# Stage one of the first two batches as plain products over 94 input rows, in place of folded rows of 120

## The chip, the cores and the metric

One core of one Trainium2 chip. The metric is the device time of one execution in microseconds; the kernel before took 2572.51 us, the median of three runs (2570.09 to 2573.17). Less is better.

## The reference

An input x of 8 batches x 3008 positions x 256 channels, float32, goes through a frequency-domain layer and then through a two-matrix feed-forward layer:

```python
X = np.fft.rfft(x, axis=1)
Yr = Xr @ w_r - Xi @ w_i + b_r
Yi = Xr @ w_i + Xi @ w_r + b_i
Yr = np.sign(Yr) * np.maximum(np.abs(Yr) - 0.01, 0.0)     # Yi likewise
y = np.fft.irfft(Yr + 1j * Yi, n=3008, axis=1)
h = y.reshape(24064, 256) @ w_in
out = (np.maximum(h, 0.0) ** 2) @ w_out
```

`w_r` and `w_i` are 256 x 256, `w_in` is 256 x 2048, `w_out` 2048 x 256; the last two are given in double precision and used as sums of two reduced-precision parts.

## The kernel before

**The transform.** 3008 is 64 x 47 (N1 x N2). Stage one is a transform of length 47 over n2 for each of the 64 values of n1; of the 47 outputs 24 groups g are kept, since the others mirror them. Stage two is, for each group, a product with a 128 x 128 matrix (`bm`) over n1 and the two parts (t: cosine and sine sums). Mixing with `w_r` and `w_i`, the bias, the threshold and the way back follow, group by group. Between the stages the data go through DRAM: `s1` holds the result of stage one, `s3` that of the first half of the way back.

**Folding.** In stage one x(n2) and x(47 - n2) share a cosine and differ in the sign of the sine. So the host lays 24 pairs out side by side, and a tile has 120 rows (24 pairs x 5 values of n1, M1) and 13 tiles (J) per batch. `Fwd32` (L429, batch 0) loads two tiles together, adds and subtracts the pair on DVE and POOL (`fold`, L276), multiplies the sum and the difference by the cosine and sine halves of `am32` (L444, products of 512 columns over both tiles), copies to `xe` with ACT and DVE and stores to `s1` (`store`, L282) on SP's queue. `Fwd2` (L406, batch 1) does not fold: it multiplies both members of the pair and adds in PSUM, by `am32` or by its negative `nam`, four products of 256 columns per tile, and copies with ACT over the tile that it read. `Fwd` (batches 2 to 7) folds on POOL and multiplies in split precision.

**The order of the work.**
- *Front* (L784 to L800). SP loads `am32` and the tiles of batch 0, four at first, each further one when a buffer (`big`) comes free. `awake` (L126) gives TensorE products on zeros: 6 at the start, 16 behind the last product of stage one. Behind the last store `load_mix_weights` (L134) loads the mixing weights and the first `kbb` on SP's queue, and splits the weights with ACT and DVE.
- *Units* (L819 to L839). `Unit32` is one group of batch 0: `load` reads `ka` from `s1`, `fwd` (L477) is stage two, `mix` (L491), `shrink` (threshold, `kv`), `back` (L503), `store`; the calls are staggered over five rounds. Beside them DVE and ACT convert the feed-forward weights: 16 parts of 512 KB (`Double`), of which `paced` takes parts 0 to 8 at a rate of one per 2.5 units, with `win_sums` after parts 1, 5, 9 and 13. Parts 9, 10, 12 and 13 (`BEHIND`) are loaded in the last units and converted behind them; 11, 14 and 15 (`LATE`) are converted within the first seven steps (`turns`). In rounds 12 to 18 `load_early` fetches seven tiles of batch 1 (`PRE`), whose stage one runs directly behind the units (L840), with stores on POOL's queue.
- *Main part.* A new pool `main` takes the memory of the closed ones. The first token tile's way back (`Back.mm`, banks `psfa` and `psfb`), its split into `yt`, and two more tiles of batch 1 come first. Then 384 steps follow (48 token tiles x 8), each 21 products `psh` of the first matrix and 12 products `pso` of the second. DVE combines `psh` (`mp`, `mu`, `mv`, `mc`), ACT squares and rounds, DVE or POOL takes the rest (`mg`). A planner (`Plan`, L689) places everything else of the transform into the slots between, two PSUM banks wide: the last four tiles of batch 1 (L920), the groups of batch 1 (`Pair`, from slot 14.8 on), stage one of batch 2 and on.

`then` (L574) chains the instructions of one engine in program order, `load_next` (L116) those of a DMA queue; `issue_after` puts an instruction behind another one on the same engine. Otherwise the order on an engine is set when the program is built.

## Time and profile before

| what | value |
|---|---|
| median of three runs | 2572.51 us |
| the profiled execution's own time | 2569.69 us |
| its span (first to last instruction) | 2567.9 us |
| TensorE (PE) busy | 2554.5 us, 99% |
| VectorE (DVE) busy | 1809.3 us, 70% |
| ScalarE (ACT) busy | 1369.7 us, 53% |
| GpSimd (POOL) busy | 1616.9 us, 63% |
| DMA | 244.47 MB, mean 95 GB/s |

Busy times are of the span. Products are pipelined and their ends are modelled, so a busy TensorE is not one at its peak, and a float32 product stands as two records. PEld is the weight load, SPq the queue of DMA issues that SP runs, POOLq that of POOL. A line of the order of time gives start, duration, engine, line, operation, output<-input, shape, count, and in brackets the idle time ahead of it with what ended it. "KB" of a transfer is 1024 bytes; GB/s are 10^9 bytes.

### The profile page before, as it was taken

Reading aid. Unit: us, or ns where it says so; the run is one execution under the profiler, and the core shown is the slowest. Engines: PE = TensorE matmul, PEld = TensorE weight load, DVE = VectorE, ACT = ScalarE, POOL = GpSimd, SP = SyncE. Lnnn points to the kernel's source line nnn. Section 1 sums busy time; section 2 is a strip of 40 time slices with the busy share of each in tenths; the row PEclk is TensorE's granted clock in tenths of the full one; section 3 lists DMA queues with packets and bytes.
Section 4 is the critical chain, followed back from the end, with each engine's and each line's share of the span. In section 5 each row is a group of like instructions: output and inputs, shape, how many; then the busy total and the mean of one; then the engine's idle time right before and its main releaser. Section 6 shows DMA issues by size and latency. Waiting matters only on the chain.

```text
span 2567.9 us, 47397 instructions
## 1 busy us (share of the span) xinstructions
PE 2554.5 (99%) x17140; PEld 2347.1 (91%) x17140; DVE 1809.3 (70%) x3808; ACT 1369.7 (53%) x2178; POOL 1616.9 (63%) x1604
## 2 busy tenths in 40 slices
PE   9999999999999999999999999999999999999999
PEld 6899999999999999999999999999999999999998
DVE  6887776777757876678766787667776667756554
ACT  5755555555555555555555555555555555545453
POOL 1056666676666766676666766666666666756564
PEclk9999999999999999999999999999999999999999
DMA  9633333333323332233322333223332232211010
GB/s 278 223 89 108 104 91 89 115 99 102 95 77 98 102 114 85 82 105 117 103 79 77 112 106 103 80 79 111 105 114 84 66 94 83 65 45 54 22 35 17
DMA packets 184715, 244.47 MB, mean 95 GB/s; under 512 B 20934, under 2 KB 130102, under 8 KB 184482
## 3 DMA queue, kind: packets, MB, share of 16 engines
q1 hardware_dynamic: 171442, 217.10, 27.5%
q0 software_dynamic: 13040, 24.34, 3.8%
q8 instruction: 137, 2.24, 0.4%
q14 instruction: 96, 0.79, 0.1%
HBM read 143.97 MB, written 97.39 MB: 94 GB/s over the span
## 4 chain that ended last, share of the span: by engine, by line
PE 96%; DVE 1%; POOL 1%; DMA 1%; issue 1%; ACT 0%; SPq 0%; POOLq 0%; ACTq 0%; DVEq 0%
PE pso L576 40%; PE psh L576 36%; PE psfa L576 9%; PE psfb L576 9%; PE psf L491 2%; PE psf L576 0%; PE psf L477 0%; PE psf L503 0%; DMA x<-x_in 0%; DMA xt<-x_in 0%; DVE mc L108 0%; POOL mg L111 0%; DMA w<-w_r_in 0%; PE psf L444 0%; DVE mv L576 0%
## 5 line engine op out<-in xcount | busy, mean ns | idle before, releaser
L111 POOL TENSOR_TENSOR mg<-mc,mg 128x500 fp32r<-128x500 f32 (+1 forms) x756 | 955.2, 1285 | 597.3 <-ACT mg L104 502.4
L576 PE MATMUL pso<-mg,wout 128*128 128x500 f32 (+1 forms) x4608 | 1153.6, 391 | 0.4 <-ACT mg L104 0.2
L576 PE MATMUL psh<-yt,win 128*128 128x250 f32 (+1 forms) x8064 | 1040.8, 280 | 1.0 <-DVE mc L108 0.9
L576 PEld LDWEIGHTS psh<-yt,win 128*128 128x128 f32 x8064 | 989.5, 189 | 13.2 <-PE psh L576 0.8
L576 PEld LDWEIGHTS pso<-mg,wout 128*128 128x128 f32 x4608 | 821.3, 188 | 132.5 <-POOL mg L111 1.3
L576 ACT ACTIVATE mc<-mc 128x1000 f32<-128x1000 f32 (+1 forms) x384 | 400.9, 1044 | 490.5 <-DVE mc L108 488.6
L108 DVE CUSTOM_DVE_ANT_0 mc<-psh,mv 128x500 f32<-128x500 f32 (+3 forms) x768 | 419.1, 548 | 345.0 <-PE psh L576 303.2
L104 ACT CAST mg<-mc 128x1000 fp32r<-128x1000 f32 (+1 forms) x384 | 396.5, 1032 | 20.3 <-ACT mc L576 0.4
L576 DVE TENSOR_TENSOR mv<-psh,mu 128x500 f32<-128x500 f32 (+1 forms) x384 | 260.8, 679 | 34.6 <-PE psfb L576 0.5
L105 DVE COPY mp<-psh 128x250 f32<-128x250 f32 (+1 forms) x376 | 157.0, 418 | 57.9 <-PE psh L576 37.2
L278 POOL TENSOR_TENSOR xs<-xt 120x256 f32<-120x256 f32 x156 | 112.5, 742 | 103.5 <-DMA xt<-x_in 89.2
L576 DVE TENSOR_TENSOR mu<-psh,mp 128x250 f32<-128x250 f32 (+1 forms) x384 | 160.4, 418 | 15.1 <-ACT mp L104 4.7
L108 DVE CUSTOM_DVE_ANT_0 mc<-psh,mp 128x250 f32<-128x250 f32 (+1 forms) x384 | 156.9, 408 | 0.0
L111 POOL TENSOR_TENSOR ksl<-kv,ksh 128x512 fp32r<-128x512 f32 x84 | 109.1, 1299 | 27.3 <-ACT ksh L104 20.7
L111 DVE TENSOR_TENSOR ul<-xs,uh 120x512 fp32r<-120x512 f32 x78 | 91.7, 1175 | 32.6 <-ACT uh L104 31.5
L111 POOL TENSOR_TENSOR yt<-ms,yt 128x500 fp32r<-128x500 f32 (+1 forms) x94 | 107.4, 1143 | 1.3 <-ACT yt L104 1.3
L111 POOL TENSOR_TENSOR yt<-yr,yt 128x500 fp32r<-128x500 f32 (+1 forms) x95 | 89.5, 942 | 21.3 <-ACT yt L104 17.7
L111 POOL TENSOR_TENSOR ms<-yr 128x250 f32<-128x250 f32 (+1 forms) x94 | 65.4, 703 | 52.3 <-DVE yr L563 37.0
L104 ACT CAST ksh<-kv 128x512 fp32r<-128x512 f32 x84 | 52.2, 621 | 76.1 <-DVE kv L111 76.1
L389 DVE TENSOR_TENSOR kv<-psfb,ke 64x256 f32<-64x256 f32 x184 | 77.5, 421 | 14.1 <-PE psfb L576 11.0
L111 POOL TENSOR_TENSOR kyl<-kp,kyh 128x256 fp32r<-128x256 f32 x84 | 62.4, 743 | 35.8 <-ACT kyh L104 35.6
L104 ACT CAST uh<-xs 120x512 fp32r<-120x512 f32 x78 | 48.3, 619 | 57.6 <-DMA s<-xe 40.8
(167 smaller groups left out, 2960.8 us busy)
## 6 DMA issues: line engine op xcount, KB each, us to landing
du<-s SPq DMA_DIRECT2D x112, 256.0 KB, 3.1
ka<-s SPq DMA_DIRECT2D x84, 256.0 KB, 3.5
kcm<-cm_in POOLq DMA_DIRECT2D x84, 256.0 KB, 3.1
s<-kuh SPq DMA_DIRECT2D x168, 128.0 KB, 1.7
s<-kul SPq DMA_DIRECT2D x168, 128.0 KB, 2.0
xt<-x_in SPq DMA_DIRECT2D x84, 240.0 KB, 3.5
s<-xe SPq DMA_DIRECT2D x79, 240.0 KB, 2.4
out<-mo SPq DMA_DIRECT2D x64, 250.0 KB, 3.1
```

The lines of the kernel that those rows point to most:

```text
L104: return act.copy(out=out, in_=in_)
L105: return eng.tensor_copy(out=out, in_=in_)
L108: return dve._custom_dve(TENSOR_ADD_SAT, out=out, in0=in0, in1=in1, s0=_float(0x7F7FFFFF), s1=0.0)
L111: return eng.tensor_tensor(out=out, in0=a, in1=b, op=ALU.subtract)
L278: return eng.tensor_tensor(out=out[:, :n], in0=self.xt[:, :n, 0], in1=self.xt[:, :n, 1], op=(ALU.add, ALU.subtract)[t])
L389: dve.tensor_add(out=v[64 * r:64 * r + 64, g], in0=ps[gs], in1=self.e[gs, r])
L491: nc.tensor.matmul(ps[:, :D], self.x[:, c, js], w32[j][:, c], start=n == 0, stop=n == 3)
L576: last_of[eng] = op(*args, **kwargs)
```

## The change

- Batches 0 and 1 get a stage one without pairs. The host lays x out as 96 rows (K1): two halves of n1 (32 values each) by 47 values of n2, and two rows of zeros. One 96 x 96 matrix `am` gives all 24 groups, both parts and both halves in one product. A `Block` is four n1 (JB): 96 x 1024, 384 KB, two products of 512 columns, two copies back into the tile that was read, one store. Eight blocks (NB) make a batch. `s1` of these batches has 128 rows per group in the order of part and n1, and stage two uses `bt`, the matrix `bm` with its rows in that order.
- Batch 0: all eight loads are issued at once (eight buffers `x4`, the first block in two loads); the mixing weights' loads stand behind blocks 3 and 4. ACT copies the first bank and DVE the second. Behind the store of block 1 SP loads `kbb`, behind that of block 3 part 0 of the feed-forward weights; the biases `b32` go on POOL's queue. `awake` behind the last product has 8 products in place of 16.
- Part 0 is converted ahead of the units, parts 1 to 8 one round earlier than before, and part 9 within the units (round 21); `BEHIND` is 10, 12, 13.
- Batch 1: six blocks are loaded in rounds 10 to 20 into `x4`, multiplied behind the units, copied by ACT and stored on POOL's queue; the pool `early` that holds them is closed after them. The remaining two blocks are four `Half`s of 96 x 512 behind the first way back. The planner gets no tile of batch 1, and `nam` goes.

The diff, cut to its core:

```diff
+K1, JB = 2 * N2 + 2, 4
+NB = N1 // 2 // JB
 FRONT = {
-    "a32": 1, "b32": 1, "w320": 1, "w321": 1, "big": 4, "small": 4, "ds": 1, "dw": 3, "ka": 6, "xe": 7, "x2": 4,
-    "kv": 4, "kc": 2, "kn": 2, "kx": 3, "ku": 4, "psf": 6, "x6": 7, "nam": 1, "zero": 1,
+    "b32": 1, "w320": 1, "w321": 1, "big": 4, "small": 4, "ds": 1, "dw": 3, "ka": 6, "x4": 8,
+    "kv": 4, "kc": 2, "kn": 2, "kx": 3, "ku": 4, "psf": 6, "zero": 1,
...
-    s1 = [dram.tile([G, NP1, 2, D], F32, name=f"s1_{b}") for b in range(B)]
+    s1 = [dram.tile([G, NP1, 2, D] if b > 1 else [G, 2 * N1, D], F32, name=f"s1_{b}") for b in range(B)]
...
-    am32 = const.tile([M1, 2, M1], F32, name="am32")
+    am = const.tile([K1, K1], F32, name="am")
...
-    nc.sync.dma_start(am32, a32)
+    nc.sync.dma_start(am, a96)
...
-    def load_mix_weights():
+    def load_bias():
         b32 = T("b32", [128, D], F32)
         for j, v in enumerate((b_r, b_i)):
-            with tc.issue_after(ring[5].folds[1].ins):
-                pool.dma_start(b32[64 * j:64 * j + 64, :], v.unsqueeze(0).broadcast_to([64, D]))
-        for j, w in enumerate((w_r, w_i)):
-            st = T(f"w32{j}", [128, 2, D], F32)
-            w32.append(st)
-            nc.sync.dma_start(st, w.rearrange("(c p) d -> p c d", p=128))
-        Unit32.matrix(0, "kbb", bm)
+            pool.dma_start(b32[64 * j:64 * j + 64, :], v.unsqueeze(0).broadcast_to([64, D]))
+        return b32
+
+    def load_mix(j):
+        st = T(f"w32{j}", [128, 2, D], F32)
+        nc.sync.dma_start(st, (w_r, w_i)[j].rearrange("(c p) d -> p c d", p=128))
+        return st
+
+    def split_mix():
...
             self.a = T("ka", [128, 2, D], F32)
-            load_next(self.a, s1[self.b][self.g:self.g + 2, :N1].rearrange("g n t c -> (n t) g c"))
+            src = s1[self.b][self.g:self.g + 2]
+            load_next(self.a, src[:, :N1].rearrange("g n t c -> (n t) g c") if self.b > 1 else src.rearrange("g n c -> n g c"))
             self.m = T("kb", [128, 2, 128], F32)
-            load_next(self.m, bm[:, self.g:self.g + 2])
+            load_next(self.m, (bm if self.b > 1 else bt)[:, self.g:self.g + 2])
...
-    class Fwd2(Fwd):
-        def load_early(self, after):
...
+    class Block:
+        def __init__(self, b, q):
+            self.b, self.q = b, q
+
+        def load(self, after=None):
+            self.xt = T("x4", [K1, JB, D], F32)
+            with tc.issue_after(after.ins) if after else nullcontext():
+                for j in range(0, JB, JB // 2) if not after and not self.q else (0,):
+                    js = slice(j, j + JB // 2) if not after and not self.q else slice(0, JB)
+                    self.get = nc.sync.dma_start(self.xt[:, js], x0[self.b, self.q, :, js])
+
+        def mm(self):
+            self.ps = []
+            for h in range(2):
+                ps = bank([128, 2, D])
+                self.end = nc.tensor.matmul(ps[:K1], am, self.xt[:, 2 * h:2 * h + 2], start=True, stop=True)
+                self.ps.append(ps)
+
+        def put(self, engs, queue):
+            for h, ps in enumerate(self.ps):
+                copy(engs[h], self.xt[:, 2 * h:2 * h + 2], ps[:K1])
+            rows = s1[self.b].rearrange("g (q j) c -> (g q) j c", j=N1 // 2)
+            self.last = queue.dma_start(rows[:, JB * self.q:JB * self.q + JB], self.xt)
+
+
+    class Half:
+        def __init__(self, q, h, tag):
+            self.q, self.j, self.tag = q, 2 * h, tag
+
+        def load(self):
+            self.xt = T("x2h", [K1, 2, D], F32, tag=self.tag)
+            load_next(self.xt, x0[1, self.q, :, self.j:self.j + 2])
 
         def run(self):
             ps = bank([128, 2, D])
...
-    class Fwd32(Fwd):
...
+            then(pe, pe.matmul, ps[:K1], am, self.xt, start=True, stop=True)
+            copy(act, self.xt, ps[:K1])
+            rows = s1[1].rearrange("g (q j) c -> (g q) j c", j=N1 // 2)
+            j = JB * self.q + self.j
+            nc.sync.dma_start(rows[:, j:j + 2], self.xt)
...
-            self.get = nc.sync.dma_start(self.a, s1[self.b][self.g, :N1].rearrange("n t c -> (n t) c"))
+            self.get = nc.sync.dma_start(self.a, s1[self.b][self.g])
...
-                        self.matrix(self.g + 1, "kbb", bm)
+                        self.matrix(self.g + 1, "kbb", bt)
...
-    ring = [Fwd32(0, q, 2) for q in range((J + 1) // 2)]
+    ring, second = ([Block(b, q) for q in range(NB)] for b in range(2))
...
-    pools.update(dict.fromkeys(("xe", "x2"), memory(early, "early", side="right")))
-    for f in ring[:FRONT["big"]]:
+    pools["x4"] = memory(early, "early", side="right")
+    for q, f in enumerate(ring):
+        if q in (4, 5):
+            with tc.issue_after(ring[q - 1].get.ins):
+                w32.append(load_mix(q - 4))
         f.load()
     awake(6)
+    behind = {2: lambda: Unit32.matrix(0, "kbb", bt), 4: parts[0].load}
     for r in range(len(ring) + 1):
+        at(ring, r, "mm")
         if r:
-            at(ring, r - 1 + FRONT["big"], "load")
-        at(ring, r, "mm")
-        at(ring, r - 1, "put")
-    awake(16, ring[-1].end)
-    early.close()
-    del pools["xe"], pools["x2"]
-    with tc.issue_after(ring[-1].last.ins):
-        b32 = load_mix_weights()
-    nam = T("nam", [M1, M1], F32)
-    act.mul(nam, am32[:, 1], -1.0)
+            f = ring[r - 1]
+            f.put((act, dve), nc.sync)
+            if r in behind:
+                with tc.issue_after(f.last.ins):
+                    behind[r]()
+            if r == 5:
+                with tc.issue_after(f.last.ins):
+                    b32 = load_bias()
+    awake(8, ring[-1].end)
+    split_mix()
     phase["pool"] = memory(middle, "middle", side="right")
...
-    PACED, BEHIND, LATE = 9, (9, 10, 12, 13), (11, 14, 15)
...
+    PACED, BEHIND, LATE = 10, (10, 12, 13), (11, 14, 15)
...
-    paced = [(n, (5 * n) // 2) for n in range(PACED)]
-    loads = [(max(k - 4, 3 * n - 3) if n < 2 else k - 4, parts[n]) for n, k in paced] + [(18 + j, parts[n]) for j, n in enumerate(BEHIND)]
-
-    PRE = 7
-    second = [Fwd2(1, q) for q in range(J)]
+    paced = [(0, -4)] + [(n, (5 * n) // 2 - 1) for n in range(1, PACED)]
+    loads = [(max(k - 4, -2), parts[n]) for n, k in paced[1:]] + [(18 + j, parts[n]) for j, n in enumerate(BEHIND)]
+
+    PRE = 6
+    halves2 = [Half(PRE + j // 2, j % 2, tag) for j, tag in enumerate(("xt", "xt", "xe", "mg1"))]
     for r in range(-5, len(units) + 4):
         at(units, r + 5, "load")
         at(units, r + 1, "fwd", "bins")
@@ -835,12 +838,15 @@
         for n, k in paced:
             if k == r:
                 convert(n, units[k - 4] if k > 3 else None)
...
-        if 0 <= r - 12 < PRE:
-            second[r - 12].load_early(units[min(r + 5, len(units) - 1)].get)
-    for q in range(PRE):
-        second[q].run()
+        if r >= 10 and not r % 2 and r // 2 - 5 < PRE:
+            second[r // 2 - 5].load(units[min(r + 5, len(units) - 1)].get)
+    for f in second[:PRE]:
+        f.mm()
+        f.put((act, act), pool)
     chain[nc.sync], chain[pool] = units[-1].get, last_pool
     middle.close()
+    early.close()
+    del pools["x4"]
     front.close()
...
-    nam = T("nam", [M1, M1], F32)
-    act.mul(nam, am32[:, 1], -1.0)
-    for f in second[PRE:PRE + 2]:
+    for f in halves2:
         f.load()
...
-    for c, f in enumerate(second[PRE:PRE + 2]):
-        at_bank[0] = ("psfa", "psfb")[c]
+    for c, f in enumerate(halves2):
+        at_bank[0] = ("psfa", "psfb")[c % 2]
         f.run()
...
-                old = run = None
-                for q in range(PRE + 2, J):
-                    at = 1.5 * (q - PRE - 2) + 1.0
-                    plan.job(max(at - 1.5, 0.6), second[q].load, [(old, 1)])
-                    old, run = run, plan.group(at + 1.5, second[q].run, 1, [(run, 3)])
                 plan.job(first - 0.6, pairs[1][0].load)
...
+    al = np.zeros((K1, G, 2, 2))
...
+        for r in range(2):
+            al[N2 * r:N2 * r + N2, g, 0, r], al[N2 * r:N2 * r + N2, g, 1, r] = np.cos(ang), -np.sin(ang)
...
+    xl = np.zeros((2, K1, N1 // 2, D), x.dtype)
+    xl[:, :2 * N2] = x[:2].reshape(2, N2, 2, N1 // 2, D).transpose(0, 2, 1, 3, 4).reshape(2, 2 * N2, N1 // 2, D)
...
-        "x0_in": np.concatenate([xi[0, :, :, q:q + 2].reshape(-1, 2, D) for q in range(0, J, 2)]),
-        "x_in": xi[1:].transpose(0, 3, 1, 2, 4, 5).reshape(B - 1, J, M1, 2, D),
+        "x0_in": xl.reshape(2, K1, NB, JB, D).transpose(0, 2, 1, 3, 4),
+        "x_in": xi[2:].transpose(0, 3, 1, 2, 4, 5).reshape(B - 2, J, M1, 2, D),
...
+        "bt_in": bm.reshape(G, N1, 2, 128).transpose(2, 1, 0, 3).reshape(128, G, 128).astype(np.float32),
```

## Rows read from the trace of the kernel before

**Rows 1.** The page, chain that ended last: share of the span by engine

```profile
PE 96%; DVE 1%; POOL 1%; DMA 1%; issue 1%; ACT 0%; SPq 0%; POOLq 0%; ACTq 0%; DVEq 0%
```

**Rows 2.** Windows: us, busy PE, PEld, DVE, ACT, POOL (instructions), clock, DMA share, GB/s

```profile
4.00:16.00 12.00, 11.27 (x24) 4.06 (x23) 5.64 (x9) 2.93 (x5) 5.30 (x3) 1.00 1.01 243
16.00:20.00 4.00, 3.96 (x10) 1.31 (x9) 2.00 (x5) 1.76 (x3) 3.05 (x4) 1.00 0.96 385
22.00:27.00 5.00, 5.00 (x25) 4.41 (x24) 0.00 (x0) 0.00 (x0) 0.00 (x0) 1.00 0.93 316
34.00:40.60 6.60, 6.60 (x38) 5.98 (x37) 6.34 (x16) 5.30 (x17) 0.00 (x0) 1.00 1.06 377
40.00:80.00 40.00, 40.00 (x217) 36.00 (x216) 39.09 (x91) 34.19 (x95) 0.00 (x0) 1.00 0.90 277
80.00:94.50 14.50, 13.21 (x67) 11.48 (x66) 9.12 (x22) 9.65 (x29) 0.00 (x0) 1.00 0.60 199
86.50:88.00 1.50, 1.50 (x10) 1.40 (x9) 1.03 (x3) 0.80 (x4) 0.00 (x0) 1.00 0.86 326
94.50:106.60 12.10, 12.10 (x57) 10.26 (x57) 10.97 (x25) 8.37 (x15) 3.21 (x6) 1.00 0.73 243
140.00:157.00 17.00, 16.63 (x104) 14.80 (x103) 15.50 (x25) 9.18 (x13) 6.40 (x7) 1.00 0.30 82
```

**Rows 3.** The front in order of time; last line: `ka`, issue to landing

```profile
1.11 5.43 PE L130 MATMUL psf<-zero 128*128 128x256 f32 x12 [1.11 <-POOL lam L123]
...
12.13 0.33 SPq L288 DMA_DIRECT2D s<-xe  x1
...
21.11 7.07 PE L130 MATMUL psf<-zero 128*128 128x256 f32 x32
...
26.64 1.30 SPq L467 DMA_DIRECT2D ka<-s  x3
...
30.05 1.13 PE L477 MATMUL psf<-kbb,ka 128*128 128x128 f32 x8 [1.87 <-ACT wx L104]
...
DMA to landing us min/median/max: 3.2/5.1/5.5
```

**Rows 4.** The chain in order of time: stage one of batch 1

```profile
94.71 12.10 PE psf L576 x56
```

**Rows 5.** Order of time from the last unit on

```profile
94.01 0.70 PE L503 MATMUL psf<-kv,kk 128*128 128x256 f32 x2 [1.29 <-DVE kv L111]
...
107.32 0.31 ACT L856 ACTIVATE nam<-am 120x120 f32<-120x120 f32 x1
```

**Rows 6.** DVE in order of time, two successive steps

```profile
148.29 0.42 DVE L576 TENSOR_TENSOR mu<-psh,mp 128x252 f32<-128x252 f32 x1 [0.49 <-ACT mp L104]
...
154.60 0.42 DVE L576 TENSOR_TENSOR mu<-psh,mp 128x252 f32<-128x252 f32 x1 [0.49 <-ACT mp L104]
```

**Rows 7.** One line's products in the front; groups from 94.5 to 106.8 us

```profile
L444 PE MATMUL psf<-x,am x28: 379/592/690, 6.5 to 20.9; 120*120 120x512 f32 x24, 120*120 120x256 f32 x4
...
L576 PE MATMUL psf<-x,am 120*120 120x256 f32 x42 | 10.2, 379 | 0.0
L104 ACT COPY x<-psf 120x512 f32<-120x512 f32 x6 | 3.5, 584 | 2.7 <-PE psf L576 2.7
```

**Rows 8.** DMA issues: count, KB each, median us to landing

```profile
s<-xe SPq DMA_DIRECT2D x79, 240.0 KB, 2.4
...
s<-x POOLq DMA_DIRECT2D x7, 240.0 KB, 5.8
...
du<-s SPq DMA_DIRECT2D x4, 192.0 KB, 2.7
```

**Rows 9.** Groups from 94.5 to 106.8 us: operations of the conversion

```profile
L176 DVE SCALAR_TENSOR_TENSOR df<-da,df 128x512 int32<-128x512 int32 x4 | 2.7, 686 | 0.0
L165 ACT ACTIVATE da<-dst 128x512 f32<-128x512 f32 x4 | 2.6, 678 | 0.0
...
L173 DVE TENSOR_SCALAR da<-da 128x512 f32<-128x512 f32 x4 | 1.7, 422 | 1.1 <-ACT da L165 1.1
```

More of the change, by code (lines that the diff above doesn't have):

```diff
@@ L42 @@
     "xs": 1, "xe": 1, "du": 2, "kv": 1, "kp": 1, "kq": 1, "ksh": 1, "ksl": 1, "kxl": 1, "kxh": 1, "kyh": 1, "kyl": 1, "ke": 1, "kb": 1, "yr": 1,
-    "amr": 1, "ms": 1, "mp": 1, "mu": 1, "mv": 1, "mc": 3, "nam": 1,
+    "amr": 1, "ms": 1, "mp": 1, "mu": 1, "mv": 1, "mc": 3,
 }
@@ L60, in fnet_moe @@
 @with_exitstack
-def fnet_moe(ctx: ExitStack, tc, x0, x, w_r, w_i, b_r, b_i, w_in, w_out, bm, cm, dx, a32, ar, c32, d32, out):
+def fnet_moe(ctx: ExitStack, tc, x0, x, w_r, w_i, b_r, b_i, w_in, w_out, bm, bt, cm, dx, a96, ar, c32, d32, out):
     nc = tc.nc
@@ L150, in load_mix_weights @@
             sub(dve, wx[1][:, j], w, wx[0][:, j])
-        return b32
     class Double:
@@ L273, in load @@
             self.xt = T("xt", [M1, 1, 2, D], F32)
-            load_next(self.xt[:, 0], x[self.b - 1, self.q])
+            load_next(self.xt[:, 0], x[self.b - 2, self.q])
         def fold(self, eng, out, t):
@@ L403, in back @@
             store_back(self.b, self.g + g, ps[:, :D])
-    class Fwd2(Fwd):
-        def load_early(self, after):
-            self.xt = T("x6", [M1, 1, 2, D], F32)
-            with tc.issue_after(after.ins):
-                nc.sync.dma_start(self.xt[:, 0], x[self.b - 1, self.q])
-        def add(self):
-            pass
+    class Block:
[18 more added lines that the diff above has]
+            self.last = queue.dma_start(rows[:, JB * self.q:JB * self.q + JB], self.xt)
@@ L415, in run @@
+    class Half:
[4 more added lines that the diff above has]
+            load_next(self.xt, x0[1, self.q, :, self.j:self.j + 2])
         def run(self):
             ps = bank([128, 2, D])
-            for t in range(2):
-                for i in range(2):
-                    then(
-                        pe, pe.matmul, ps[:M1, t], nam if t and i else am32[:, t], self.xt[:, 0, i],
-                        start=i == 0, stop=i == 1,
-                    )
@@ L423, in run @@
-            self.ev = self.xt
-            copy(act, self.ev[:, 0], ps[:M1])
-            self.store(nc.sync if self.q >= PRE else pool)
-    class Fwd32(Fwd):
-        alone = property(lambda self: self.q in (4, 8))
-        def load(self):
-            self.xt = T("x4", [M1, 2, 2, D], F32, tag="big")
-            src = x0[self.q * M1:(self.q + self.n) * M1].rearrange("(m n) t d -> m n t d", n=self.n)
-            self.get = nc.sync.dma_start(self.xt[:, :self.n], src)
-        def mm(self):
-            n = self.n
-            self.ps, self.folds = [], []
-            for t, eng in enumerate((dve, dve if self.alone else pool)):
-                u = T("x2", [M1, 2, D], F32)
-                self.folds.append(self.fold(eng, u, t))
-                ps = bank([128, 2, D])
-                self.end = nc.tensor.matmul(ps[:M1, :n], am32[:, t], u[:, :n], start=True, stop=True)
-                self.ps.append(ps)
-        def put(self):
-            self.ev = T("xe", [M1, 2, 2, D], F32)
-            for t, ps in enumerate(self.ps):
-                self.done = copy((act, act if self.alone else dve)[t], self.ev[:, :self.n, t], ps[:M1, :self.n])
-            self.last = self.store()
+            then(pe, pe.matmul, ps[:K1], am, self.xt, start=True, stop=True)
@@ L1003, in _consts @@
             cm[g, j, 64 + n1], cm[g, 64 + j, 64 + n1] = sg * w * s, sg * w * e * c
-    return am.reshape(M1, 2, M1), bm, cm, dm
+    return am.reshape(M1, 2, M1), al.reshape(K1, K1), bm, cm, dm
 def _r12(v):
```

4 lines of the change are left out of this document (2 added, 2 removed).

## The prediction

> **What bounds the kernel now.** I read the page first, then busy time by windows, then the order of time on each engine around the places that the diff touches. The page says that the end hangs on TensorE: 96% of the chain that ended last [rows 1]. From about 157 us on the diff touches nothing, so the question is how much earlier or later that steady part begins. Ahead of it lie four stretches with four limits.
>
> *Front, 0 to 30 us: transfers.* The DMA share is 0.93 to 1.01. Until 16 us, when almost only loads of x have moved, the rate is 243 GB/s; while the stores of stage one drain it is 385 [rows 2]. The first store is issued at 12.13 us, yet the rate rises only when the loads are through, so I take SP's queue as served in order. SP issues the first `ka` at 26.64 us, when the last store has landed, and units begin at 30.05 [rows 3].
>
> *Units, 30 to 94.7 us: TensorE,* busy 40.0 of 40 us in their middle, with DVE at 39.1 [rows 2]; one gap of 1.3 us at the end [rows 5].
>
> *Second batch's stage one, 94.7 to 106.8 us: TensorE,* 56 records in 12.10 us, 0.216 us each [rows 4]. Two more tiles run behind the first back products; then the steps start.
>
> *First steps, 113.8 to 157 us: VectorE, not TensorE.* A step's second half ends with an `mc`; then ACT can copy `mp` (one buffer), then DVE starts the next `mu`. That costs a wait of 0.49 us a step, and DVE is otherwise full: 15.5 of 17.0 us [rows 2], 6.31 us from one `mu` to the next [rows 6]. TensorE's 99% hides that here; its busy time is modelled.
>
> **The change, part by part.**
>
> *Stage one of batch 1 on TensorE.* Now 13 tiles of four products of 256 columns, two records each: 13 x 8 x 0.216 = 22.5 us. After: 16 products of 512 columns. A record of 512 columns lasts 0.592 us at the median in the front, one of 256 columns 0.379 [rows 7], of which 0.379 - 0.216 = 0.163 is the modelled tail; so 0.429 is its own, and a product 0.858 us. Where the 16 fall:
> - Six blocks in the bounding stretch: 12 x 0.858 = 10.3 against 12.1 us. **Gain 1.8 us.**
> - Four halves behind the back products: 3.43 against 2 x 1.73 = 3.46. Nothing.
> - The four tiles planned into the steps (6.9 us of TensorE) vanish where DVE is the limit. I cost this at nothing: the next `mu` waits for `mc`, not for a product. A loss is excluded, since work only goes; the most it could give is the 0.5 us of one wait.
> - `nam` is no longer built between the copies that the back products wait for: 0.31 us at 107.32 [rows 5]. **Gain 0.2 us.**
>
> The evictions of the six blocks are all ACT's, 12 x 0.58 = 7.0 us [rows 7] in 10.3. It has 8.4 us of work in that stretch now [rows 2]; six copies more add 3.5, part 9 takes away five operations of up to 0.68 [rows 9], some 2.9: 9.0, which fits, and six banks cover a late copy.
>
> *Part 9 into the units, part 0 ahead of them.* A part is on DVE three operations of 0.42 us and three of 0.69 [rows 9], 3.3 us; part 9 has four sums (0.42) and four differences (one of 0.42, three of 0.69) besides, 4.2. DVE has 5.4 us free from 80 to 94.5 us [rows 2], and part 0 leaves 3.3 us earlier in the units: 7.5 fits into 8.7, tightly. If the last units' `kv` operations queue behind it, they lose at most two of 0.69 us. The 7.5 us that DVE saves after the units bound nothing, since the six blocks use no DVE. Zero, at worst -1.4.
>
> *SP and POOL queues.* The units carry six loads of 384 KB for seven of 240 KB, and one part of 512 KB less: +0.1 MB on a stretch at 277 GB/s that reaches 377 [rows 2], wanted only at its end; zero. POOL issues six stores instead of seven. `du` still stands ahead of the halves' loads.
>
> *The front.* The folds go, but they only stood between landing and product. TensorE: the six opening products hold it until 6.5 us [rows 3]; 16 x 0.858 = 13.7 more, so its last product ends at 20.2 at the earliest, the last copy at 20.9, the last store is issued at 21.2. With the 2.4 us in which a 240 KB store lands in the main part [rows 8] that is 23.6: the floor. Over it stands what the queue must move by then: loads 3.15 (x) + 0.52 (mixing weights) + 0.04 + 0.23 (POOL's two constants) + 0.13 (biases) = 4.07 MB; then stores 3.15, `kbb` 0.26, part 0 0.52 = 3.93 MB. Stores go at 385 GB/s: 10.2 us. Loads of 96 partitions have no row; the ends are 243 (loads of x) and 377 GB/s (34 to 40.6 us, when no store is out). The nearest in row length, with no x beside it, is the lone part at 86.5 to 88 us, 4 KB rows at 326 [rows 2]; I take that. Loads from 2.0 us then end at 14.5, and the last store lands at 14.5 + 10.2 + 0.3 = 25.0; `ka` is issued 0.3 later. It lands in 3.2 us at best now [rows 3], with weights still in the queue; 192 KB on a quieter queue take 2.7 [rows 8], which I take. Units begin at 28.0. **Gain 2.0 us** (ends: 377 gives the floor, 23.6 + 3.0 = 26.6, +3.4; 243 gives 32.2, -2.2). Splitting the mixing weights hides in this wait.
>
> *TensorE's clock.* [...] The longest idle time ahead of the units is 1.9 us now, at a granted clock of 1.00. After, eight products fill 20.2 to 23.7 us and the engine idles to 28.0: 4.3 us, which no row shows. The price is between 0 and 5.43 - 12 x 0.22 = 2.8 us; units fill slowly at first, so I take 0.3.
> [...]
>
> *Sum.* 1.8 + 0.2 + 2.0 - 0.3 = 3.7 us. The profiled execution took 2569.69 us (span 2567.9 and 1.8 around it) and would take 2566.0; it lies 2.8 below the median of the runs, 2572.51, against which I predict: **2568.8 us**, 0.14% less. About 0.2%, 5.1 us, is what a measurement of this kernel can tell from no change: below 2567.4 or above 2577.7.
>
> **The rivals.**
>
> *Loads at full rate (0.36).* If x comes in at 377, TensorE is the front's limit, units start at 26.6 (+3.4), the engine idles only 2.9 us and keeps its clock. With 2.0 from batch 1: 5.4 us, 2567.1; the gap of 1.3 us at the units' end may be filled too, since the new products are in no chain: 2565.8. For it: the rate at 34 to 40.6 us. Against it: 12 us of x at 243.
>
> *96 partitions move slower (0.14).* Loads at 243 and the rest at the 316 GB/s of 22 to 27 us [rows 2]: 2.0 + 16.7 + 12.4 + 0.3 + 0.3 + 2.7 = 34.4, units 4.4 us late; 2.0 gained and up to 2.8 lost by the clock: 2574.9 to 2577.7. For it: x never came faster. Against it: stores of the same tiles did 385.
> [...]
>
> *Buffers freed late (0.11), slower.* The `early` pool, which holds x4, is now closed only after the six blocks, and tiles of the main part take its memory. If `du`'s place is under the last block, its load waits for that store: issued about 104, 5.8 us to land on POOL's queue, then 2.7 for `du` [rows 8]: 112.5, where the back products want it at 103.1. That is 9.4 us, and about 2 of clock behind it: 2580.2. It decides if more than 8.9 us are lost. Against it: seven tiles of the same kind stand in freed memory now, and their last stores delay no back product.
>
> **How the numbers follow.** Forecast 0.39 (0.05 of it beyond 2567.4), full rate 0.36, slow 96 partitions 0.14 (0.03 beyond 2577.7), buffers 0.11. Faster by over 0.2%: 0.36 + 0.05 = 0.41. Slower: 0.11 + 0.03 = 0.14. Within: 0.45. The range runs from 2564.0 (full rate, gap filled, and the runs' own scatter of 1.5 to 3 us in part) to 2575.5; outside lie the buffers and half of the slow case.
>
> **What would show it.** Right: the second batch's six blocks take about 10.3 us; `mu` to `mu` in the steps stays at 6.3 us although TensorE has gaps; the first unit at 26.6 to 28.0 after a DMA share near 1. Wrong: a rate under 243 or over 377 while x loads; opening records of the units twice as long; a wait of `du`, `yr` or `yt` on stores of x4; steps shorter than 6.3 us, which would mean that the four tiles did bound them.

## The result: 0.8% slower

The changed kernel took 2592.05 us, the median of six runs (2589.92 to 2597.22); the kernel before took 2571.70 beside it (2570.09 to 2573.17). The ratio is 1.0081, with a 95% interval of 1.0068 to 1.0094. The forecast was 2568.8, with a range to 2575.5. The profiled execution took 2589.92 us, its span 2588.2: 20.3 more than before. In order of time, from the first start of what is named:

| stretch | before | after | difference |
|---|---|---|---|
| start to the first unit's product | 30.05 | 31.83 | +1.8 |
| from there to the second batch's six blocks (seven tiles) | 64.50 | 66.94 | +2.4 |
| from there to the first way back | 12.09 | 10.30 | -1.8 |
| from there to the first `mu` | 8.52 | 18.08 | +9.6 |
| first to 11th `mu` | 64.13 | 64.66 | +0.5 |
| 11th to last `mu` | 2374.27 | 2381.84 | +7.6 |
| last `mu` to the end | 14.35 | 14.51 | +0.2 |

**Front.** Windows of the kernel after, which answer to [rows 2] (columns as there):

```profile
4.00:8.00 4.00, 4.00 (x11) 2.41 (x9) 0.00 (x0) 1.44 (x2) 0.00 (x0) 1.00 0.96 249
8.00:12.00 4.00, 3.63 (x9) 1.14 (x8) 0.69 (x1) 0.15 (x1) 0.00 (x0) 1.00 1.16 266
12.00:16.00 4.00, 2.82 (x7) 0.82 (x6) 1.29 (x2) 1.58 (x3) 0.00 (x0) 1.00 1.06 271
16.00:20.00 4.00, 3.56 (x9) 1.22 (x8) 3.56 (x6) 2.67 (x5) 0.00 (x0) 1.00 1.01 330
28.00:34.00 6.00, 2.17 (x9) 2.20 (x10) 2.37 (x5) 1.04 (x4) 0.00 (x0) 0.71 0.67 190
34.00:40.00 6.00, 6.00 (x25) 5.20 (x25) 1.40 (x4) 2.65 (x9) 0.00 (x0) 0.72 0.95 309
115.00:130.00 15.00, 7.88 (x40) 5.63 (x41) 6.92 (x14) 5.03 (x10) 1.98 (x2) 0.77 0.43 144
```

The DMA engines are full (share 0.96 to 1.16) while only 249 to 271 GB/s move until 16 us; behind that it is 330, against 385 before. The last of x landed at 19.85 us (before: 18.62), where the prediction let the loads end at 14.5. The order of time beside it, for [rows 3]:

```profile
16.44 0.69 DVE L113 TENSOR_TENSOR wd<-w,w 128x512 f32<-128x512 f32 x1 [0.64 <-DMA w<-w_i_in]
17.17 0.62 ACT L106 CAST wx<-wd 128x512 fp32r<-128x512 f32 x1 [1.73 <-DVE wd L113]
17.92 5.36 PE L425 MATMUL psf<-x,am 96*96 96x512 f32 x12 [0.44 <-ACT wx L106]
21.08 4.86 SPq L432 DMA_DIRECT2D s<-x  x4
23.11 3.62 PE L132 MATMUL psf<-zero 128*128 128x256 f32 x16
29.77 1.76 SPq L465 DMA_DIRECT2D ka<-s  x4
31.83 2.04 PE L475 MATMUL psf<-kbb,ka 128*128 128x128 f32 x8 [5.10 <-DMA ka<-s]
```

The last twelve records (a product is two) run from 17.92 to 23.28; the prediction had the last product at 20.2. ACT and DVE split the mixing weights between the copies, waiting for `w`. Ahead of the units TensorE idles 5.1 us, and the granted clock of the windows at 28 and 34 us is 0.71 and 0.72: in windows of 0.5 and 1 us it is 0.50 to 0.52 from 30.5 to 37 us, and 1.00 ahead of that and from 37.5 us on.

**Second batch.** Pieces of the chain of waits, in order of time:

```profile
24.07 5.49 DMA s<-x
...
98.94 10.32 PE psf L425 x24
110.15 8.47 DMA s<-x
```

The six blocks take 10.32 us against 12.10 [rows 4] (their first product starts at 98.77, the chain's row 0.17 later). Then the chain goes through a store. The order of time behind it:

```profile
110.15 0.51 POOL L432 DMA_DIRECT2D s<-x  x1 [1.21 <-ACT yr L106]
...
118.80 0.42 DVE L113 TENSOR_TENSOR yt<-yr,yt 128x252 fp32r<-128x252 f32 x1 [9.90 <-DMA s<-x]
118.93 1.40 POOL L113 TENSOR_TENSOR yt<-yr,yt 128x504 fp32r<-128x504 f32 x1 [8.28 <-DMA s<-x]
...
120.97 0.61 ACT L106 CAST yt<-ms 128x504 fp32r<-128x504 f32 x1 [7.48 <-DVE ms L113]
...
121.49 0.57 ACT L106 COPY x2h<-psfa 96x512 f32<-96x512 f32 x1
...
122.11 2.02 PE L574 MATMUL psfa<-x2h,am 96*96 96x512 f32 x2 [7.80 <-ACT x2h L106]
...
127.15 0.42 DVE L574 TENSOR_TENSOR mu<-psh,mp 128x252 f32<-128x252 f32 x1 [3.86 <-ACT mp L106]
```

`yt` is split into a rounded part and a low part. The low part of the first `yt` lies where the last block was, and waits for that block's store to land. `ms` (sums of the way back's results) stands behind it on DVE, ACT's cast waits for `ms`, ACT's copy of `x2h` (the tile of a half block) stands behind the cast, and TensorE waits for the bank. When it goes on, the two records of a half block take 2.02 us, at a granted clock of 0.50 (120 to 126 us); two such records took 1.08 at 112.38, at 1.00.

### The profile page after: what moved, and what is told of

The parts are those of the page before. It is cut to its first block, busy times and chain, and to the rows that moved or that the text cites. A ratio compares the mean times of both kernels' runs of the same rounds, so it can differ in the third digit from the quotient of the medians.

```text
span 2588.2 us, 47216 instructions
## 1 busy us (share of the span) xinstructions
PE 2558.0 (99%) x17056; PEld 2340.2 (90%) x17056; DVE 1811.8 (70%) x3802; ACT 1370.9 (53%) x2178; POOL 1613.0 (62%) x1598
## 4 chain that ended last, share of the span: by engine, by line
PE 94%; DVE 2%; DMA 2%; POOL 1%; issue 1%; ACT 1%; SPq 0%; POOLq 0%; ACTq 0%; DVEq 0%
PE pso L574 39%; PE psh L574 35%; PE psfa L574 9%; PE psfb L574 8%; PE psf L489 2%; PE psf L425 1%; DMA s<-x 1%; PE psf L475 0%; DMA w<-w_i_in 0%; PE psf L501 0%; DVE mc L110 0%; DMA s<-xe 0%; POOL mg L113 0%; DMA xt<-x_in 0%; DVE mg L113 0%
## 5 line engine op out<-in xcount | busy, mean ns | idle before, releaser
L106 ACT CAST yt<-ms 128x500 fp32r<-128x500 f32 (+1 forms) x96 | 58.6, 611 | 45.3 <-POOL ms L113 37.4
```

Of the source, the lines that this page charges most:

```text
L106: return act.copy(out=out, in_=in_)
```

## The experiments

All times are beside runs of the kernel before on the same chip, 2569.67 to 2571.70 in the median. "Six blocks" is the start of their products, "ten steps" the time from the first to the 11th `mu` (64.13 before). The kernels e5 to e7, e9 to e15 and e18 keep the blocks out of `yt`'s way, as e1 does. The stretches of a row come from one trace. Kernels with the same front start their units up to 1.2 us apart: 31.23 to 32.25 in six with the changed front (changed kernel, e1, e4, e5, e9, e12), 28.86 to 30.05 in four with the front of before (before, e8, e16, e17). A difference of two traces below that tells little.

| run | first unit | six blocks | first `mu` | ten steps | 11th to last `mu` | time us | ratio (95%) |
|---|---|---|---|---|---|---|---|
| changed kernel | 31.83 | 98.77 | 127.15 | 64.66 | 2381.84 | 2592.05 | 1.0068 to 1.0094 |
| e1_place | 31.23 | 98.15 | 117.96 | 64.70 | 2383.46 | 2583.16 | 1.0035 to 1.0061 |
| e2_split | 31.49 | 98.76 | 129.22 | 65.00 | 2385.20 | 2594.28 | 1.0072 to 1.0100 |
| e3_part0 | 33.60 | 100.79 | 129.31 | 65.35 | 2383.63 | 2593.60 | 1.0073 to 1.0100 |
| e4_awake | 32.25 | 97.86 | 128.26 | 64.78 | 2381.92 | 2591.78 | 1.0067 to 1.0094 |
| e5_nam | 31.66 | 97.83 | 117.62 | 64.65 | 2381.97 | 2581.75 | 1.0031 to 1.0056 |
| e6_pool | 31.36 | 98.53 | 118.38 | 64.61 | 2381.69 | 2580.00 | 1.0022 to 1.0047 |
| e7_all | 30.95 | 97.73 | 117.52 | 64.65 | 2381.86 | 2581.47 | 1.0030 to 1.0055 |
| e9_same | 32.13 | 99.06 | 118.84 | 65.01 | 2380.75 | 2580.82 | 1.0029 to 1.0054 |
| e10_pace | 32.08 | 98.46 | 121.38 | 69.22 | 2377.26 | 2584.14 | 1.0044 to 1.0070 |
| e11_both | 31.78 | 97.34 | 121.52 | 68.93 | 2380.25 | 2586.39 | 1.0048 to 1.0075 |
| e12_plan | 32.23 | 98.88 | 117.68 | 64.77 | 2378.86 | 2577.63 | 1.0015 to 1.0036 |
| e13_wlate | 29.17 | 96.74 | 116.76 | 65.74 | 2378.95 | 2579.75 | 1.0020 to 1.0045 |
| e14_front | 29.71 | 94.94 | 115.83 | 68.70 | 2378.72 | 2579.56 | 1.0021 to 1.0048 |
| e15_sum | 30.23 | 96.93 | 115.73 | 65.29 | 2376.50 | 2575.23 | 1.0008 to 1.0026 |
| e18_last | 28.33 | 95.36 | 115.49 | 70.23 | 2382.40 | 2580.55 | 1.0022 to 1.0050 |
| before + 32 bytes (e8_shift) | 29.68 | 94.83 | 115.44 | 64.19 | 2379.57 | 2574.98 | 1.0008 to 1.0026 |
| before + 64 bytes (e17_shift64) | 28.86 | 94.63 | 115.24 | 64.21 | 2377.99 | 2574.37 | 1.0006 to 1.0024 |
| before again (e16_again) | 29.95 | 94.45 | 115.05 | 64.11 | 2375.40 | 2570.83 | 0.9993 to 1.0010 |

### The blocks' place

```diff
+            self.tag = f"x4{AT[q] if b else q}"
...
+    AT = (2, 0, 6, 7, 1, 4, 3, 5)
```

> Only the places of the second batch's six blocks change: the last two (stored at 108.4 and 110.2 us) lie under tiles that the main part first writes for its second token tile, not under yt1 of the first. Theory 'memory': yt waits for no store, the first mu comes at 115.2 + 4.2 (units' end) - 1.8 (six blocks) - 0.2 = 117.4 us in place of 127.15, TensorE keeps a clock of 1.00 between 115 and 130 us, and the time falls by 9.8 us to about 2582. Rival 'queues': the wait is POOL's slow queue and ACT's order (the copies of x2h behind the casts to yt), whatever lies where: mu stays at 125 to 127 us and the time at 2590 to 2592.

The rows of e1_place that answer to the stall (window, DVE, TensorE):

```profile
115.00:130.00 15.00, 13.43 (x94) 11.96 (x94) 11.45 (x24) 9.59 (x20) 0.99 (x2) 1.00 0.55 177
```

```profile
111.00 0.42 DVE L113 TENSOR_TENSOR yt<-yr,yt 128x252 fp32r<-128x252 f32 x1 [2.72 <-ACT yt L106]
...
113.92 1.10 PE L575 MATMUL psfa<-x2h,am 96*96 96x512 f32 x2 [0.22 <-ACT x2h L106]
115.71 1.10 PE L575 MATMUL psfb<-x2h,am 96*96 96x512 f32 x2 [0.69 <-ACT x2h L106]
...
117.96 0.42 DVE L575 TENSOR_TENSOR mu<-psh,mp 128x252 f32<-128x252 f32 x1 [2.07 <-ACT mp L106]
```

'Memory' holds. From the first way back to the first `mu` 9.51 us are left of 18.08: the place cost 8.6 us, the slow clock behind it included. The 1.0 us more than the 8.52 before stand in the two TensorE rows: four half blocks on two banks wait for copies that stand behind casts on ACT. e12_plan, which gives these products back to the planner, takes 8.50.

### The front

Splitting the weights behind the copies:

```diff
-        sub(dve, wd, w32[1], w32[0])
...
+        a, v = (c.ins for c in ring[-1].put_by)
+        with tc.issue_after(v):
+            sub(dve, wd, w32[1], w32[0])
...
```

> Only the splitting of the mixing weights moves: ACT and DVE do it behind the last copies of stage one, not between them. Theory 'evictions': the products of the front end at 21.5 in place of 23.3 us, the last store lands at 27.8 in place of 29.6 and the first unit starts at 30.0 in place of 31.8: -1.8 us. Rival 'transfers': the DMA engines are full from 4 to 28 us already (share 0.96 to 1.16), so the products end earlier but the last store lands within 0.5 us of 29.6: 0 to -0.5 us.

'Transfers' holds: the first unit, at 31.49, lies among the six kernels with the changed front, and nothing was gained in time. The waits of `wx` in the rows looked like the cause and were not.

Part 0 behind the last store, `behind = {2: ..., 8: parts[0].load}`:

> Only the load of weight part 0 moves from behind the store of block 3 to behind the last store. Theory 'transfers': 0.52 MB at the 343 to 376 GB/s of 20 to 28 us leave the stretch ahead of the last landing, which comes at 28.1 in place of 29.6 us; the first unit starts 1.5 us earlier, unless the later conversion (it then runs beside the first units) takes part of that back. Rival 'evictions': the last store waits for the last copy, so nothing ahead of 24 us changes and the landing gains less than 0.5 us.

Neither holds: the first unit came 1.8 us later. Part 0 now stood between the last store and `ka` on SP's queue, and in this execution x came in more slowly (230 GB/s from 8.25 to 16.5 us, against 270 in the changed kernel) and the last twelve records began only at 20.01 (17.92), which part 0 can't explain. It tells little; e10 below is the better test.

More products on zeros, `awake(16, ...)` for 8:

> Only the products on zeros behind stage one change, 16 in place of 8: TensorE is busy to about 30.3 us and idles 1.5 us ahead of the units in place of 5.1. Theory 'clock': the stretch at half the clock from 31 to 38 us goes, and the units end 2.0 to 2.4 us earlier (last product at 96 in place of 98.24): time -2.2 us. Rival: the first units are bound by loads of ka and by DVE, so a clock of 1.00 there moves the units' end by less than 0.5 us.

Windows and the first unit of e4_awake:

```profile
28.00:34.00 6.00, 4.23 (x23) 3.39 (x22) 2.71 (x6) 1.43 (x5) 0.00 (x0) 1.00 0.62 192
34.00:40.00 6.00, 6.00 (x34) 5.21 (x33) 1.25 (x4) 2.25 (x6) 0.00 (x0) 1.00 0.99 326
```

```profile
32.25 1.15 PE L475 MATMUL psf<-kbb,ka 128*128 128x128 f32 x8 [1.77 <-DMA ka<-s]
```

Here 1.8 us are idle, the granted clock is 1.00 in both windows, and the units take 97.86 - 32.25 = 65.6 us in place of 66.9. So the slow clock costs some 1.3 of the 2.4 us (in e1, e5, e9 and e12, whose first eight records take 2.04 or 2.05 us as in the changed kernel, 1.15 here, they take 66.2 to 66.9); the other 1.1 are not settled. The time as a whole moved by no more than its scatter.

Holding POOL's four loads back, with a small POOL copy from block 5 ahead of them:

> As e1_place, but POOL's four loads (two biases, two constants; 0.35 MB) wait until block 5 of the first batch is copied out, where the changed kernel issues them at 1.3 to 3.6 us beside the loads of x. Theory 'bias': those loads hold up the DMA engines (share 0.96 while only 249 GB/s move from 4 to 8 us); without them x arrives 2 us earlier and the first unit starts at 29.8 in place of 31.8 us: -2 us against e1_place. Rival 'x itself': loads of x go at 243 to 271 GB/s whatever runs beside them, as in the kernel before, and 0.35 MB moved behind them give 1.3 us there and cost 0.9 us in the stores: -0.4 us at best.

'x itself' holds: the first unit at 31.36 against 31.23, and 240 to 250 GB/s from 4 to 16 us again.

Mixing weights and `kbb` behind the last store (on e9_same):

```diff
-            with tc.issue_after(ring[q - 1].get.ins):
-                w32.append(load_mix(q - 4))
...
+    with tc.issue_after(ring[-1].last.ins):
+        w32.extend(load_mix(j) for j in range(2))
+        Unit32.matrix(0, "kbb", bt)
```

> e9_same with the loads of the mixing weights and of the first kbb behind the last store, as before the change. Theory 'slow loads': while x comes in everything that is loaded beside it goes at about 250 GB/s, so 0.52 MB of mixing weights hold x up by 2 us; without them the last three blocks start at 16 in place of 18 to 19 us, the last store lands at 28 in place of 29.6 and the first unit starts at 31 or before (e9_same 32.8 by the same count): -1.5 to -2 us. Rival 'bytes': what is taken from the front of the queue comes back behind it, the first unit waits for the weights instead: 0 to +1 us.

Windows of e13_wlate, and its products in order of time:

```profile
8.00:12.00 4.00, 3.59 (x9) 1.39 (x10) 0.88 (x2) 1.16 (x2) 0.00 (x0) 1.00 1.13 273
12.00:16.00 4.00, 4.00 (x11) 1.38 (x10) 1.68 (x3) 1.16 (x2) 0.00 (x0) 1.00 1.04 263
16.00:20.00 4.00, 4.00 (x11) 1.55 (x10) 1.75 (x3) 1.18 (x3) 0.00 (x0) 1.00 1.02 394
```

```profile
8.41 12.40 PE L426 MATMUL psf<-x,am 96*96 96x512 f32 x28 [0.94 <-DMA x<-x_in]
...
29.17 1.19 PE L476 MATMUL psf<-kbb,ka 128*128 128x128 f32 x4 [4.90 <-DMA ka<-s]
```

'Slow loads' holds: the first unit at 29.17, and at 30.23 in e15_sum, which has the same loads, against 31.23 to 32.25; some 2 us for 0.52 MB of mixing weights and 0.26 MB of `kbb`. The last of x landed at 17.66 and 18.64 us, against 19.50 to 20.53 in those six. No window of 4 us from 4 to 16 us moved more than 273 GB/s (before, changed kernel, e6, e9, e10 and e13), so bytes beside x hold it up; from 20 to 24 us, when x had landed and stores moved with one weight part, it was 420 here. The products run through to 20.8 us, close to the 20.2 that the prediction called the floor, and the first unit comes about as early as with the front of before. Why loads are slow while x arrives, the runs don't tell.

### The weight parts, and what becomes of an earlier end

Part 0 in the units and part 9 behind them, as before the change (on e9_same; `PACED` is 9 again, and part 0 is not loaded ahead of the units):

```diff
-    paced = [(0, -4)] + [(n, (5 * n) // 2 - 1) for n in range(1, PACED)]
+    paced = [(n, (5 * n) // 2) for n in range(PACED)]
```

> e9_same with the weight parts paced as before the change: part 0 in the units, no part ahead of them, part 9 behind them. Theory 'bytes': 0.52 MB fewer ahead of the last store's landing, at 343 to 420 GB/s, start the first unit 1.3 us earlier (30.6 in place of 31.9 us), and the units end 1.3 to 2 us earlier, at 97; part 9's 4.2 us on DVE behind the units cost nothing. Rival 'x': the loads of x set the front, and the first unit moves by less than 0.5 us; and a third way, part 9 delays the first casts to yt and takes back 1 to 2 us.

'Bytes' falls: 0.52 MB fewer ahead of the units changed the first unit by 0.05 us. Part 0 moves among the stores, where 412 and 407 GB/s go from 20 to 28 us (e9_same). The third way holds: the first `mu` came 2.5 us later. The ten steps behind it took 69.22 us in place of 65.01, which no theory had; e14_front below shows why. With the split and 16 products on top:

> e10_pace with the mixing weights split behind the copies and 16 products on zeros. Theory 'clock': the granted clock stays at 1.00 from the units on, the first product of a unit's way back comes 8 us behind the first forward product (10.2 in the changed kernel, 7.8 before) and the units end 2 us earlier than in e10_pace: time -2. Rival: -1.3 at most, as between e4_awake and the changed kernel from first unit to last; or nothing, if the weights' split now stands in front of the first units' copies on ACT.

The six blocks started 1.1 us earlier and the first `mu` no earlier at all. With the planner's four tasks back (e12, below) and nearly the whole front as before:

> e12_plan with the front in the order of the kernel before: mixing weights and kbb behind the last store, biases held until block 5 is copied, part 0 in the units, part 9 behind them, 16 products on zeros; only the blocks of 94 rows are left of the change. If each cause adds up: first unit at 30 to 30.5, clock 1.00, units' end at 95 in place of 99.5 us, six blocks at 10.3: 4.5 us less than e12_plan, 2569.5 if 'phase' holds there, 2575 if not. Rival: part 9 behind the units delays the first yt as in e10_pace (2.5 us), and the time is 2572 to 2577.

The units ended as early as hoped, the rest did not follow. DVE and TensorE of e14_front in order of time, and two of its waits from 95 to 180 us (engine, line, what it waited for, total, times, longest):

```profile
109.75 0.69 DVE L197 TENSOR_TENSOR dw<-dw,df 128x512 f32<-128x512 f32 x1
...
110.36 1.46 DVE L114 TENSOR_TENSOR yt<-yr,yt 128x252 fp32r<-128x252 f32 x1
...
111.87 0.58 PE L576 MATMUL psh<-yt,win 128*128 128x252 f32 x1 [2.39 <-DVE yt L114]
...
115.83 0.42 DVE L576 TENSOR_TENSOR mu<-psh,mp 128x252 f32<-128x252 f32 x1 [1.07 <-ACT mp L107]
```

```profile
POOL amr L121 <- DVE dw L191: 14.7, 1, 14.7
PE psfb L576 <- DMA kb<-bt_in: 3.1, 1, 3.1
```

With part 9 behind the units DVE converts until 110.4, whatever TensorE saves: from the six blocks' start to the first `mu` it is 20.89 us, against 20.61 before. With part 9 within the units, in e12_plan and e15_sum, it is 18.80: there TensorE's 1.8 us arrive whole.

The larger loss lies in the ten steps, 68.70 us against 64.77 in e12_plan. The loads of the second batch's first pair (`amr`, `ka`, `kb`) are issued only at 159 to 160 us, 14 us later than before, when the last weight part is converted, and TensorE waits 3.1 us for `kb`. e10, e11 and e18 have the same (68.93 to 70.23 us). These are the four versions that convert part 0 in the units; in their programs these three lie where the conversion's `da` and `df` of the last parts are, in e12_plan, e15_sum and before the change in a `dst` that an earlier part used. So this is a matter of places too. Without the 3.9 us e14_front would come to 2575.6, an estimate. One edit more, part 9 back in the units:

> e14_front with one edit: part 9 is converted within the units again (round 22), as the change does. Theory 'DVE behind the units': in e14_front the units end at 94.9 us but the first yt waits for DVE, which converts until 110.3; with part 9's 4.2 us moved ahead, the first way back starts at 105.2 and the first mu comes 8.5 us later, at 113.7 (e14_front 115.83, before 115.16), and the time falls by 2 to 3 us, to 2577; with the 2376.5 us of e15_sum behind the 11th mu it would be 2572. Rival: DVE has no room for 4.2 us more in the last units, whose kv then comes late: units' end at 96 to 97, first mu at 115 to 116, time unchanged.

The rival holds: the units started at 28.33 but took 67.0 us, the wait for `kv` at their end was 1.78 us (1.29 in e14_front), the granted clock was 0.83 from 90 to 100 us, the six blocks took 11.60 us in place of 10.32, and the first `mu` came at 115.49. Beside part 0 DVE has no room for part 9 in the units. The time is no better than that of e14_front above all for the ten steps, 70.23 us.

### Behind the 11th mu

TensorE issues the same products there in the same order. First `nam`'s 480 bytes as an unused tile:

> As e1_place, and nam's 480 bytes come back in the main pool as an unused tile, so that every later tile of the main part lies 480 bytes higher, an odd multiple of 32, as it lay before the change. From the 11th mu to the last one the kernel before takes 2374.3 us, the changed one 2381.8 and e1_place 2383.5, with the same order of instructions on TensorE. Theory 'addresses': that stretch returns to 2374 to 2376 us and the time falls by 8 to 9 us against e1_place, to about 2574.5. Rival 'stalls': the stretch is longer through collisions that begin with another phase of the planned tasks; it stays at 2381 to 2385 and the time at 2581 to 2585.

No change in the stretch, though the other tiles were not yet where they had been. Then the reverse, in the kernel before, `T("nam", [M1, 128], F32)[:, :M1]`:

> The kernel before, with nothing changed but the width of nam: 512 bytes in place of 480, so that every later tile of the main part lies 32 bytes higher. Theory 'addresses': the stretch from the 11th mu to the last grows from 2374.3 to 2381 to 2384 us and the time from 2570.8 to 2578 to 2581. Rival 'stalls': both stay, 2374 and 2570 to 2572.

32 bytes cost the kernel before 0.17% (0.08 to 0.26), and the stretch takes 5.3 us more. With 64:

> The kernel before with nam's tile 544 bytes wide: every later tile of the main part lies 64 bytes higher (32 in e8_shift). Theory 'alignment to 64 bytes': as before, 2374 us in the stretch and 2570 to 2572 in all. Theory 'any other place': 2377 to 2381 us in the stretch, 2573 to 2577 in all.

0.15% (0.06 to 0.24), so not the alignment to 64 bytes. All four levers together, on e5_nam:

> e5_nam, e6_pool, the split of the mixing weights behind the copies and 16 products on zeros together. Theory (places of x4, addresses, transfers and clock each as measured or expected alone): 2574.5 - 2.0 - 0.5 - 1.3 = 2570.7 us, level with the kernel before. Rival 'stalls' and 'x itself': 2583 - 0.4 - 0.5 - 1.3 = 2581 us.

The second forecast held: the clock is 1.00 from 30 to 42 us, but ACT waited 4.3 us for a weight part in the first units, and the stretch stayed. Then every tile at its earlier address (unused tiles that hold the order of places):

> The changed kernel with every tile of the constants and of the main part at the address that it had before the change (am's tile wide again, nam's place kept, the order of tiles as before), and the second batch's blocks placed so that no tile of the first steps waits for their stores. Theory 'addresses', after 32 bytes cost the kernel before 4.7 us: the stretch from the 11th to the last mu returns to 2374 to 2376 us (e1_place 2383.5, e5_nam 2382.0), and the time falls to 2574 to 2576. Rival 'stalls' (the four tiles that left the planner shift the phase of what follows): 2380 to 2383 us and a time of 2580 to 2583.

The stretch stayed here too, at 2380.75. And the planner's four tasks given back, the half blocks all in the buffers `xt`:

> e9_same with the last four half blocks given back to the planner, in the slots that the four tiles of the kernel before had, in place of four products behind the first way back. Theory 'phase': the planned tasks behind them fall as before, the stretch from the 11th to the last mu returns to 2374 to 2377 us (e9_same 2380.75), the first step starts 1 us earlier since no product waits for a copy of x2h, and the time falls from 2580.8 to 2574. Rival 'layout or chance': the stretch stays at 2380 to 2383 and the time at 2578 to 2580.

The stretch came down by 1.9 us, not to 2374 to 2377. Finally the kernel before once more:

> The kernel before once more, unchanged. If the stretch from the 11th to the last mu is a property of the program, it takes 2374 to 2375 us again; if collisions in it fall out differently from one execution to the next, it takes anything up to 2380, and the 4.6 us of e12_plan and e14_front there need no cause in the change. The ratio should be 1.000 within 0.1%.

What settles it is the end of the stretch, where the planner has little left. The 299th and the 383rd `mu`, DVE in order of time, of before, after, e9_same, e12_plan and e8_shift:

```profile
2065.39 0.42 DVE L576 TENSOR_TENSOR mu<-psh,mp 128x252 f32<-128x252 f32 x1
...
2548.43 0.42 DVE L576 TENSOR_TENSOR mu<-psh,mp 128x250 f32<-128x250 f32 x1
```

```profile
2084.41 0.42 DVE L574 TENSOR_TENSOR mu<-psh,mp 128x252 f32<-128x252 f32 x1
...
2568.49 0.42 DVE L574 TENSOR_TENSOR mu<-psh,mp 128x250 f32<-128x250 f32 x1
```

```profile
2075.74 0.42 DVE L575 TENSOR_TENSOR mu<-psh,mp 128x252 f32<-128x252 f32 x1
...
2559.45 0.42 DVE L575 TENSOR_TENSOR mu<-psh,mp 128x250 f32<-128x250 f32 x1
```

```profile
2073.14 0.42 DVE L575 TENSOR_TENSOR mu<-psh,mp 128x252 f32<-128x252 f32 x1
...
2556.18 0.42 DVE L575 TENSOR_TENSOR mu<-psh,mp 128x250 f32<-128x250 f32 x1
```

```profile
2069.88 0.42 DVE L576 TENSOR_TENSOR mu<-psh,mp 128x252 f32<-128x252 f32 x1
...
2554.04 0.42 DVE L576 TENSOR_TENSOR mu<-psh,mp 128x250 f32<-128x250 f32 x1
```

483.04 us before; 484.08 after; 483.71 in e9_same; 483.04 in e12_plan; 484.16 in e8_shift. By the trace's starts it is 483.03 to 483.04 in the six kernels with all tiles at their earlier addresses (before, again, e12, e14, e15, e18), 484.08 or 484.09 in the changed kernel and the four others with its addresses, and 483.70 or 483.71 in e9, e10, e11 and e13. In those four the two buffers of `mg1` are swapped from step to step, because one half block took one of them; e12 undoes that. Three more sets of places give 484.25 (e5_nam), 483.60 (e6_pool) and 484.16 (e7_all). The windows of the 84 steps in before, after and e8_shift, columns as in [rows 2]:

```profile
2065.39:2548.43 483.04, 483.04 (x3211) 444.03 (x3211) 309.29 (x672) 238.67 (x332) 299.16 (x282) 1.00 0.17 53
2084.41:2568.49 484.08, 484.08 (x3211) 444.55 (x3211) 309.42 (x672) 238.74 (x332) 299.68 (x282) 1.00 0.17 53
2069.88:2554.04 484.16, 484.16 (x3211) 444.93 (x3210) 309.41 (x671) 238.68 (x332) 298.85 (x282) 1.00 0.17 53
```

By the profile TensorE is busy without a gap, at a clock of 1.00, with the same 3211 records; they only take longer. So these 84 steps follow the places of the tiles alone, to 0.01 us: 1.04 us, or, if all 373 steps behind the 11th `mu` lose as much, an estimate of 4.6 of the 7.6 us. Which tile's place counts, and why, the runs don't tell. The other 3 are not settled: the six kernels with equal addresses differ from 2374.3 to 2382.4 in the whole stretch, so steps that hold planned work differ besides, and e16_again shows 1.1 of that in one program.

### The sum

> e12_plan with the front of e13_wlate (mixing weights and kbb behind the last store) and 16 products on zeros; part 0 stays ahead of the units and part 9 within them, so that the conversions don't stand in front of the first yt as in e14_front. If the causes add up: first unit at 30, clock 1.00, units' end at 96 to 96.5, first mu at 115 to 116 (before: 115.6 by the same count), and only the 4 to 5 us behind the 11th mu are left: 2573 to 2575 us. Rival: as the units end earlier, another of DVE's or ACT's queues takes their place, and the first mu stays at 117.5 or later: 2577.

The best version of the change, 2575.23: 0.6% faster than the change as made, 0.17% (0.08 to 0.26) slower than the kernel before. Its first `mu` is 0.6 us late. The 1.8 us of the six blocks are in that, but the units take 66.7 us: the 16 products on zeros did not hold the clock here, which was 0.72 from 30 to 36 us behind 1.44 us of idle time. The ten steps take 1.2 us more than before and the stretch behind them 2.2. No version beat the kernel before.

## Why the prediction was wrong

- **Six blocks, 1.8 us: right.** 10.32 us where 10.3 stood; ACT's twelve copies fitted. In e12_plan and e15_sum the gain reaches the first `mu`.
- **"Buffers freed late (0.11)": this decided.** The mechanism was right and the price near (9.4 and about 2 expected, 8.6 in all measured), the victim was not: `du` came in time, the low half of `yt` was late. The step that failed is the argument against it. That seven tiles stand in freed memory now and delay nothing shows that the places happened to suit, not that any place does; which tile lies under the last block was not looked up.
- **Front, +2.0: wrong in sign, -1.8** (some 2 us by all kernels with either front). The step is the rate: 326 GB/s from a lone part; measured 249 to 271 while x arrived, next to the end of 243 that the text gave (-2.2). e13_wlate and e15_sum show the rest: the mixing weights were counted as bytes among others, but beside x they hold x up. "Splitting the mixing weights hides in this wait" did not hold in the rows, yet e2_split gained nothing by it.
 The row in question was the rate of 243 with 120 partitions, and 96 partitions were hardly different (249 to 271). With x landed, stores and one weight part moved at 420 GB/s (e13_wlate, 20 to 24 us).
- **Clock, -0.3: mis-sized, some -1.3** (e4_awake), inside the 0 to 2.8 given. The 2.8 was the author's estimate from [rows 3], 0.45 us a record at the start against 0.22 behind stage one; the granted clock of that trace is 1.00 in both places. The 0.3 no run shows: behind 5.1 us of idle time the changed kernel's clock fell to 0.50 for 6.5 us, and the price, 1.3, lies in the middle. Another 1.1 us of the units stand in no term and are open. For the idle time 4.3 us were forecast.
- **Four halves, "nothing": -1.0**, since four tiles on two banks need four copies in time where two needed two.
- **Four planned tiles, zero: near for the steps** (64.13 and 64.66 us for ten). The 0.5 us are a loss, which the text excluded "since work only goes"; their cause is open.
- **Part 9 into the units, zero:** the waits for `kv` at the units' end are 1.17 us where 1.29 stood, so it bound nothing there. But "the 7.5 us that DVE saves after the units bound nothing" is wrong: with part 9 behind the units DVE has the first `yt` in hand, and the 1.8 us are lost (e14_front, 20.89 us from the six blocks to the first `mu`, against 18.80).
- **`nam` gone, +0.2:** the copy went, and its place with it, as did the places of nearly all tiles. The step is "from about 157 us on the diff touches nothing": behind the 11th `mu`, at 192 us, the change lost 7.6 us. That the place of tiles costs anything in 384 equal steps was in no rival; 4.6 us is the estimate, the rest is open.
